# Moving the tail of each partition's last wq row onto three DMA engines, with one x_q load and separate score rows per batch

## The chip, the cores and the metric

One core of a Trainium2 chip runs the kernel. The metric is the device time of one execution in microseconds (us). Within a set both kernels ran on the same chip; in the third set 11 of the 12 runs of the kernel before are those of the second set. A span is shorter than the metric by some 1.8 us, because it counts from the first to the last instruction of the program.

In the views, PE is the matmul engine (PEld its weight loads), DVE and ACT are the vector and scalar engines, POOL is a fourth engine, and SP (SyncE) issues the large loads; a name with q behind it (SPq, ACTq) is an engine's instruction queue, and L93 is line 93 of the kernel. Apart from these there are sixteen DMA engines, here called engine 0 to 15 (the traces do not number them), which move the data. Of their queues, q1 carries the weights and caches, q10 the small x loads and the output, and q8 and q14 carry instructions.

## The reference, cut to what matters

One decode step for four sequences: layer norm, q projection, sliding-window attention over 2048 cached positions, output projection, then a gated MLP.

```python
def reference(A_x, A_k_cache, A_v_cache, A_wq, A_wo, B_x, B_w1, B_w3, B_w2):
    # B=4, D=1024, Hq=32, Hkv=4, Dh=128, W=2048, F=3584, all bf16
    xn = layernorm(A_x)
    q = xn @ A_wq                                  # wq: 1024 x 4096, 8.4 MB
    k, v = A_k_cache[:, :, -W:], A_v_cache[:, :, -W:]   # 8.4 MB each
    p = softmax(q . k * Dh ** -0.5)                # each batch has its own scores
    h = A_x + (p . v) @ A_wo                       # wo: 8.4 MB
    hn = layernorm(h)
    return h + (silu(hn @ B_w1) * (hn @ B_w3)) @ B_w2   # 7.3 MB each
```

The weights and caches are 55.6 MB, each byte is used once, and all of it must come through the DMA queue.

## The kernel before

All large loads are issued by SyncE into one SBUF ring, in the order of a plan. Partition p of the wq tile holds rows 8p to 8p+7 of wq, one after another, so the "last wq row" of a partition is row 8p+7.

```python
    def load_rows(at, src, n, r0, m):
        t = ring[:, at : at + m * n]
        nc.sync.dma_start(out=t, in_=src[:, r0 * n : (r0 + m) * n])
        return [t[:, k * n : (k + 1) * n] for k in range(m)]
    plan = [
        ("wq", load_rows, (0, wq_v, N_Q, 0, 4)),
        ("wq", load_rows, (32 * KIB, wq_v, N_Q, 4, 4)),
        ("k", load_kv, (64 * KIB, A_k_cache, 0)),
        ...
    ]
    ...
    for j in range(JG):                       # x_q: the residual, in four DMAs
        nc.scalar.dma_start(
            out=x_q[QD * j : QD * (j + 1) : RS, :], in_=x_flat[:, j * CG : (j + 1) * CG])
    ...
    for kc in range(KC):                      # q projection, KC = 8
        wq_t = loaded["wq"][kc]
        for hf in range(CQ // 512):
            for g in range(JG):               # four column groups of the array
                c0 = g * CQ + hf * 512
                nc.tensor.matmul(q_ps[QD * g : QD * g + B, hf * 512 : (hf + 1) * 512],
                    lhsT=xnT[:, kc, :], rhs=wq_t[:, c0 : c0 + 512],
                    start=(kc == 0), stop=(kc == KC - 1))
        if kc == RQ - 1:
            load_next()
    ...
            nc.tensor.matmul(                 # scores
                scores_ps[QD * g : QD * (g + 1), n * 512 : (n + 1) * 512],
                lhsT=qz[:, b, g * QD : (g + 1) * QD], rhs=kT_v[:, g, :, :],
                start=(b == 0), stop=(b == B - 1))
```

## Time and profile before

| | before |
|---|---|
| time, median of the 6 runs beside the changed kernel | 138.34 us (138.11 to 138.45) |
| span of the profiled run | 136.34 us |
| q1 packets' share of 16 engines' span | 95.3% |
| landing of the last w2 load | 132.97 us |
| landings of that load, engine by engine | eight at 131.12 to 131.62, eight at 132.35 to 132.97 us |

The prediction below shows the lines on the bound. (In its line of DMA digits each digit is the busy share of the sixteen engines in one fortieth of the span, in tenths.) Two more views matter. The first is a part of the list of DMA issues (target and source, issuing engine, count, KB each, us to landing where known), the second the waits of SyncE's own queue (who waited for what: us in total, times, longest).

```profile
ring<-in_A_wq_dram SPq DMA_DIRECT2D x2, 4096.0 KB, 16.8
...
x_q<-in_A_x_dram ACTq DMA_DIRECT2D x4, 2.0 KB
```

```profile
SPq L101 <- DMA ring<-in_A_wq_dram: 16.2, 2, 9.9
```

Line 101 issues the K and V loads. It waits for wq although K has nothing to do with wq. In the trace's instruction records each DMA posts its completion to one of eight semaphores, in turn, and a DMA whose semaphore is still in use must wait until the earlier DMA has landed. The third K load got the semaphore of the first wq load and was issued at 13.02 us, when that landed. It cost nothing, for the second wq load and two K loads were queued by then.

### The profile page before, as it was taken

How to read it: one execution, taken by the hardware profiler on the slowest of the kernel's cores; microseconds unless marked ns; L12 is line 12 of the kernel's file. 1: busy time of each engine (PE TensorE's matmuls, PEld its weight loads, DVE VectorE, ACT ScalarE, POOL GpSimd, SP SyncE). 2: the span in 40 equal slices, each digit the busy share in tenths (PEclk: the TensorE clock that was granted, in tenths of full speed). 3: DMA queues.
4: the chain of work that ended last, by engine and by line, in shares of the span. 5: the costliest groups of instructions: out<-in, count | busy, mean ns of one | idle time of the engine just before them, and what ended most of it. 6: DMA issues, size and time to landing. Idle time of an engine off the chain costs nothing.

```text
span 136.3 us, 2302 instructions
## 1 busy us (share of the span) xinstructions
PE 67.9 (50%) x1035; PEld 42.9 (31%) x1035; DVE 42.6 (31%) x73; ACT 31.0 (23%) x36; POOL 1.7 (1%) x8
## 2 busy tenths in 40 slices
PE   0101803698989889105259538830096440900960
PEld 0100201274656565001149427610043210300840
DVE  6440000244444444609940030160000695070000
ACT  0400000155555646092944000000003300000001
POOL 5000000000000000000000000000000000000000
PEclk9999999999999999965555865897557777555577
DMA  5999899999999999997988989989799999989960
GB/s 156 462 462 443 385 413 418 423 447 423 428 437 409 437 437 423 435 582 341 538 385 365 524 365 442 459 353 522 328 412 463 434 437 447 429 388 409 426 261 5
DMA packets 2662, 55.75 MB, mean 409 GB/s; under 512 B 312, under 2 KB 344, under 8 KB 604
## 3 DMA queue, kind: packets, MB, share of 16 engines
q1 hardware_dynamic: 2592, 55.58, 95.3%
q8 instruction: 8, 0.13, 0.3%
q10 hardware_dynamic: 60, 0.02, 0.1%
q14 instruction: 2, 0.02, 0.0%
HBM read 55.59 MB, written 0.01 MB: 408 GB/s over the span
## 4 chain that ended last, share of the span: by engine, by line
DMA 58%; PE 21%; ACT 13%; DVE 5%; issue 1%; SPq 0%; ACTq 0%
DMA ring<-in_B_w_dram 42%; DMA ring<-in_A_wq_dram 16%; PE kt_ps L263 9%; ACT kT L269 6%; PE scores_ps L248 5%; ACT z L304 3%; PE q_ps L215 2%; PE g_ps L403 2%; DVE rmax L280 2%; ACT Pm L285 2%; PE OT_ps L326 2%; DVE pT L294 1%; DVE z L300 1%; ACT L285 1%; DVE q_sb L225 1%
## 5 line engine op out<-in xcount | busy, mean ns | idle before, releaser
L269 ACT COPY kT<-kt_ps 128x1024 bf16<-128x1024 bf16 x16 | 15.8, 1014 | 12.0 <-PE kt_ps L263 12.0
L263 PE MATMUL kt_ps<-ident,ring 128*128 128x128 bf16 x256 | 16.4, 219 | 0.0
L263 PEld LDWEIGHTS <-ring 128*128 128x128 bf16 x256 | 14.3, 98 | 5.0 <-issue 4.9
L267 DVE COPY kT<-kt_ps 128x1024 bf16<-128x1024 bf16 x16 | 11.1, 691 | 15.2 <-PE kt_ps L263 15.2
L215 PE MATMUL q_ps<-ring,xnT 128*4 128x512 bf16 x64 | 6.7, 596 | 12.0 <-DMA ring<-in_A_wq_dram 12.0
L403 PEld LDWEIGHTS <-hnT 128*32 128x32 bf16 x128 | 5.3, 137 | 23.1 <-issue 20.5
L248 PE MATMUL scores_ps<-kT,qz 128*32 128x512 bf16 x64 | 9.9, 609 | 3.1 <-ACT kT L269 3.1
L326 PE MATMUL OT_ps<-z,ring 128*128 128x32 bf16 x256 | 7.4, 185 | 6.7 <-ACT z L304 5.0
L403 PE MATMUL u_ps<-ring,hnT 128*32 128x448 bf16 x64 | 6.3, 572 | 8.3 <-DMA ring<-in_B_w_dram 8.3
L403 PE MATMUL g_ps<-ring,hnT 128*32 128x448 bf16 x64 | 5.4, 525 | 9.0 <-DMA ring<-in_B_w_dram 9.0
L433 PE MATMUL y_ps<-ring,hgT 128*32 128x256 bf16 x112 | 5.7, 370 | 8.4 <-DMA ring<-in_B_w_dram 8.3
L326 PEld LDWEIGHTS <-ring 128*128 128x128 bf16 x256 | 7.3, 103 | 7.4 <-issue 7.4
L433 PEld LDWEIGHTS <-hgT 128*32 128x32 bf16 x112 | 4.4, 129 | 10.3 <-issue 6.1
L215 PEld LDWEIGHTS <-xnT 128*4 128x4 bf16 x64 | 2.1, 116 | 16.2 <-issue 15.9
L353 PE MATMUL y_ps<-ring,o 128*32 128x256 bf16 x128 | 5.8, 365 | 2.0 <-DMA ring<-in_A_wo_dram 2.0
L443 ACT CAST res<-y_ps 128x256 bf16<-128x256 f32 x1 | 0.4, 372 | 26.5 <-PE y_ps L433 26.5
L304 ACT ACTIVATE z<-pt_ps,mask 128x512 bf16<-128x512 f32 x8 | 5.3, 687 | 3.5 <-DVE z L300 3.5
L225 DVE TENSOR_SCALAR q_sb<-q_ps 128x512 bf16<-128x512 f32 x1 | 0.7, 690 | 17.2 <-PE q_ps L215 17.2
L353 PEld LDWEIGHTS <-o 128*32 128x32 bf16 x128 | 4.8, 130 | 3.8 <-issue 3.1
L300 DVE TENSOR_SCALAR z<-pt_ps,mask 128x512 bf16<-128x512 f32 x8 | 5.5, 740 | 1.2 <-ACT z L304 0.8
L296 PE MATMUL pt_ps<-pT,perm 128*128 128x512 bf16 x4 | 2.4, 607 | 6.8 <-DVE pT L294 6.8
L417 DVE RECIPROCAL eg<-eg 128x896 f32<-128x896 f32 x1 | 5.8, 5753 | 0.0
(73 smaller groups left out, 40.5 us busy)
## 6 DMA issues: line engine op xcount, KB each, us to landing
ring<-in_A_wq_dram SPq DMA_DIRECT2D x2, 4096.0 KB, 16.8
ring<-in_A_k_cache_dram SPq DMA_DIRECT2D x4, 2048.0 KB, 25.5
ring<-in_A_v_cache_dram SPq DMA_DIRECT2D x4, 2048.0 KB, 40.2
ring<-in_B_w_dram SPq DMA_DIRECT2D x1, 7168.0 KB
ring<-in_B_w_dram SPq DMA_DIRECT2D x2, 3584.0 KB, 28.6
ring<-in_B_w_dram SPq DMA_DIRECT2D x1, 4352.0 KB
ring<-in_B_w_dram SPq DMA_DIRECT2D x1, 1792.0 KB
ring<-in_B_w_dram SPq DMA_DIRECT2D x1, 768.0 KB
```

Of the source, the lines that this page charges most:

```text
L215: nc.tensor.matmul(q_ps[QD * g : QD * g + B, hf * 512 : (hf + 1) * 512], lhsT=xnT[:, kc, :], rhs=wq_t[:, c0 : c0 + 512], start=(kc == 0), ...
L248: nc.tensor.matmul(scores_ps[QD * g : QD * (g + 1), n * 512 : (n + 1) * 512], lhsT=qz[:, b, g * QD : (g + 1) * QD], rhs=kT_v[:, g, :, :], ...
L263: nc.tensor.transpose(out=kt_ps[:, jj, :], in_=k_v[:, n * NJ + t * TB + jj, :], identity=ident[:])
L267: nc.vector.tensor_copy(out=kT[:, t * TB : (t + 1) * TB, :], in_=kt_ps[:])
L269: nc.scalar.copy(out=kT[:, t * TB : (t + 1) * TB, :], in_=kt_ps[:])
L300: nc.vector.tensor_scalar(out=z[:, :, g, :], in0=pt_ps[:], scalar1=mask[:, g : g + 1], scalar2=None, op0=ALU.mult)
L304: nc.scalar.mul(out=z[:, :, g, :], in_=pt_ps[:], mul=mask[:, g : g + 1])
L326: nc.tensor.matmul(OT_ps[:, b, :], lhsT=loaded["v"][b][:, j, :], rhs=PTz[j // NJ][:, (j % NJ) * B + b, :, :], start=(j == 0), stop=(j == J ...
L353: nc.tensor.matmul(y_ps[QD * j : QD * (j + 1), :], lhsT=o4[:, i, :, :].rearrange("p b s -> p (b s)"), rhs=loaded["wo"][i][:, j * CG : (j + ...
L403: nc.tensor.matmul(out_ps[QD * j : QD * (j + 1), hf, :HF], lhsT=hnT[:, k, :], rhs=loaded[kind][k][:, c0 : c0 + HF], start=(k == 0), stop=( ...
L417: nc.vector.reciprocal(out=eg[:], in_=eg[:])
L433: nc.tensor.matmul(y2_ps[QD * j : QD * (j + 1), :], lhsT=hgT[:, i, :], rhs=loaded["w2"][i][:, j * CG : (j + 1) * CG], start=False, stop=(i ...
```

## The change

The intent: the completion of a load needs all sixteen DMA engines, and some have spare time at the end. So 768 B are cut from each partition's last wq row, on all engines alike, and the cut pieces (128 of them) are gathered by three DMAs whose shape confines them to engines 0 to 2. The q projection adds the gathered pieces by eleven small matmuls, which use the matching rows of xn. The x_q load becomes one DMA in place of four. The score matmul takes its weights from a window that is shifted by 8 columns per batch, so that each batch has rows of its own. (Before, the four batches were summed in the same rows; the comparison with the reference accepted both kernels.)

```diff
+    CE = 384
+    SETS = [(0, 3, 5), (60, 3, 5), (120, 2, 1)]
+    def load_side(r0, ne, ns):
+        t = ktpool.tile([P, JG * QD * 16], BF16, tag="kT")
+        rows = A_wq[r0 * KC : (r0 + ne * 4 * ns) * KC, N_Q - CE : N_Q]
+        rows = rows.rearrange("(t i k) n -> k i t n", i=ne, k=KC)[KC - 1]
+        nc.sync.dma_start(out=t[: ne * 4, : ns * CE], in_=rows)
+        return [t[: ne * 4, k * CE : (k + 1) * CE] for k in range(ns)]
+    def load_tail(at, src, n, r0, m):
+        t = ring[:, at : at + m * n]
+        nc.sync.dma_start(out=t[:, : m * n - CE], in_=src[:, r0 * n : (r0 + m) * n - CE])
...
-        ("wq", load_rows, (32 * KIB, wq_v, N_Q, 4, 4)),
+        ("side", load_side, SETS[0]),
+        ("side", load_side, SETS[1]),
+        ("side", load_side, SETS[2]),
+        ("wq", load_tail, (32 * KIB, wq_v, N_Q, 4, 4)),
...
-    for j in range(JG):
-        nc.scalar.dma_start(
-            out=x_q[QD * j : QD * (j + 1) : RS, :], in_=x_flat[:, j * CG : (j + 1) * CG]
-        )
+    nc.scalar.dma_start(out=x_q[0:P:RS, :], in_=x_flat.rearrange("b (j c) -> j b c", j=JG))
...
+    (eleven slices of xn are gathered by 3 DVE copies, transposed on PE, copied to xsT)
...
+                n = min(512, N_Q - CE - c0) if kc == KC - 1 else 512
...
         if kc == RQ - 1:
             load_next()
+            for k, np_ in enumerate(sl):
+                nc.tensor.matmul(
+                    q_ps[QD * (JG - 1) : QD * (JG - 1) + B, CQ - CE : CQ],
+                    lhsT=xsT[:np_, k, :], rhs=loaded["side"][k], start=False, stop=False)
...
-                lhsT=qz[:, b, g * QD : (g + 1) * QD],
+                lhsT=qz_v[:, z0 : z0 + QD],
```

(The line in brackets stands for the part that prepares xsT.)

## The prediction

> **What bounds the kernel now.** I read the page's head, its DMA digits and queues first, then the chain of waits, the groups, the timeline of the last stretch and the SyncE queue's own waits. The page says that DMA is busy nearly everywhere and moves 55.75 MB at 409 GB/s over the whole span:
>
> ```profile
> DMA  5999899999999999997988989989799999989960
> DMA packets 2662, 55.75 MB, mean 409 GB/s; under 512 B 312, under 2 KB 344, under 8 KB 604
> q1 hardware_dynamic: 2592, 55.58, 95.3%
> q8 instruction: 8, 0.13, 0.3%
> q10 hardware_dynamic: 60, 0.02, 0.1%
> q14 instruction: 2, 0.02, 0.0%
> ```
>
> Queue q1 carries all weights and caches: 18 DMAs of 128 rows plus one completion packet on each of 16 engines give 18 x 144 = 2592 packets. It alone fills 95.3% of the engines' span. The chain names 58% DMA, but it follows the compute in the middle; it begins and ends on DMA:
>
> ```profile
> 1.16 21.35 DMA ring<-in_A_wq_dram
> ...
> 101.59 31.37 DMA ring<-in_B_w_dram
> ...
> 133.01 0.32 PE y_ps L433 x4
> ...
> 133.35 0.37 ACT res L443
> ```
>
> Behind the last landing stand only four matmuls, one copy and the 8 KB output, so the end is the landing at 132.97 us plus about 3.4 us. In the middle, PE arrives before its data and not after it:
>
> ```profile
> PE q_ps L215 <- DMA ring<-in_A_wq_dram: 12.0, 2, 6.1
> PE g_ps L403 <- DMA ring<-in_B_w_dram: 9.0, 1, 9.0
> PE y_ps L433 <- DMA ring<-in_B_w_dram: 8.3, 3, 7.1
> PE y_ps L353 <- DMA ring<-in_A_wo_dram: 2.0, 1, 2.0
> ```
>
> And each large load is issued before the queue runs dry: the timeline has the first w1 load issued at 73.22 us, while wo, the load ahead of it, lands at 82.1 us. So the queue has 8.9 us of spare time there, and wo, issued at 39.74, still more.
>
> The deciding detail is in the trace's packet records (start, duration, size, queue; no engine number). A packet starts within some 10 ns of the end of the one before it, so they link into sixteen gap-free sequences of the same 144 q1 data packets each. Every sequence is busy from about 2 us to its end, and the ends fall into two groups: eight at 130.78 to 131.32 us and eight at 132.05 to 132.67 us. The late eight are exactly those into which an instruction packet fell before the end: seven q8 packets of 16 KB (starting at 31.2, 42.1, 52.5, 75.4, 82.2, 88.5, 106.5 us; 0.88 to 0.96 us each) and one q14 packet at 57.9 us. Each costs its engine some 1.3 us for good. The eighth q8 packet starts at 131.11 us, on an engine already done. A load has landed only when its slowest engine has, so **the latest instruction-hit engine sets the time**, and eight others idle for the last 1.3 us.
>
> **What the Trainium skill says.** "DMA: Bandwidth & Descriptors", section "Why a DMA increments its semaphore by 16 and not by 1": a DMA is split over the largest k up to 16 that divides the slowest dims of both sides, on this issue path over the lowest-numbered k engines. The trace fits: q10 has x_sb (4 data and 4 completion packets), four x_q loads (4 and 4 each) and the output (16 and 4), 8 + 32 + 20 = 60, so four-row copies run on four engines. The change's side loads have outer sizes 3 against 12, 3 against 12, and 2 against 8: engines 0 to 2, 0 to 2 and 0 to 1. Same page, "Queues, rings and completion order": an engine alternates between queues packet by packet, and completion is counted over all engines; in the trace the 512 B x_q packets start 2.45 us apart (6.04, 8.49, 10.94), always after large packets end. Same page, "Rules for kernel authors": a DMA with a small outermost size is confined to that many engines. Here that is the intent.
>
> **The change part by part.**
>
> *Bytes taken off all engines.* The second wq load shrinks by 384 x 2 = 768 B on each of 128 partitions, 8 of them per engine: 6144 B. A 32 KB packet takes 1.21 us (27.1 B per ns), so each engine ends 6144 / 27.1 = 0.227 us sooner. The packet count per engine stays 8.
>
> *Bytes put on engines 0 to 2.* The same 128 pieces come back as 60 + 60 + 8 packets of 768 B: 20 + 20 + 4 = 44 on engines 0 and 1, 40 on engine 2. For a packet this small I take the line through two sizes of this trace: successive 2048 B packets start 80 ns apart, 32,768 B ones 1211 ns, so 4.6 ns + 0.0368 ns per byte, 32.9 ns for 768 B (512 B packets took 27 ns, which agrees roughly). 44 x 32.9 = 1.45 us, with three completions of about 15 ns 1.49 us; less 0.227, **engines 0 and 1 end 1.27 us later**; engine 2, 40 x 32.9 = 1.32, plus 0.03, less 0.227: 1.12 us later. That is nearly the 1.3 us for which an engine without an instruction packet idles. So the author has filled three of the idle tails.
>
> *The end.* Engines 3 to 15: latest 132.67 - 0.23 = 132.44 us. Engines 0 to 2, if unhit: 130.78 to 131.32 plus 1.12 to 1.27, so 131.9 to 132.6 us. The sequences that carry the x_q packets, and so belong to engines 0 to 3, can be followed with some ambiguity where packets tie: three seem unhit (ends near 131.01, 131.08, 131.32), one hit. I choose to believe that engine 3 is the hit one, since the change stops at 2. Then the last data end at 132.44 to 132.59 instead of 132.67: **0.08 to 0.23 us gained, 0.15 as the middle.**
>
> *Earlier landings.* The second wq load waits for engines 0 to 2: they were somewhere in 21.98 to 22.51, and become about 23.2 to 23.7 us. The q matmuls and the whole attention start about 1.1 us later, as does the first K landing (27.4). Attention's slack against wo is 2.0 us (the wait above), so some 0.9 us is left. The w1 issue moves from 73.2 to 74.3 with 8.9 us of slack. Nothing at the end moves.
>
> *Added compute.* DVE gets three small strided copies and two out of PSUM, by the 0.17 us of the similar 128x32 copy about 0.9 us; PE eleven transposes (eight take 0.66 us, so 0.9 us). Both lie between 7.3 us and the wq landing at 13.0, where they idle. Eleven side matmuls of 384 columns share one column group: four 512-column ones side by side take 3.58 / 8 = 0.45 us, so each needs 0.34 us and all 3.7 us, from 16.6 to 20.3 us; wq1 comes after that.
>
> *x_q in one DMA.* Three issues of 0.58 us leave ACT's queue, and its table load, now at 3.94 us, starts earlier; xnT is ready at 7.2 us for data that come at 13.0. Worth nothing. With three DMAs more on SyncE the number of DMAs in this phase is the same, so the completion semaphores go round as before: SyncE holds K and V back until earlier loads have landed, but a full queue stands ahead.
>
> *Score rows.* Another 32-column slice of qz per batch: the same 64 matmuls (609 ns) and weight loads. It changes what the rows contain, not the time.
>
> **The rivals.** (1) *An instruction packet on engine 0, 1 or 2.* The mapping of sequences to engine numbers is inferred. If a hit engine is among them, it ends at 132.67 + 1.2 = 133.9 and the kernel takes about 139.6 us. The added 44 PE instructions also move the eighth q8 packet forward: it came after 2022 of 2078 instructions, and 44 earlier is near the end of the 68-matmul group (126.30 to 130.12 us), say 129.9. There its engine still has about 1 us of data; it becomes a ninth late engine, near 132.2, harmless unless it is one of 0 to 2. (2) *Small packets cost more than the line says.* At twice 33 ns the three engines end 1.45 us later still, near 134, for 139.7 us. The 27 ns of the 512 B packets speaks against it. (3) *Moved bytes hidden anyway*: if the late engines vary from run to run, the relief is just 0 to 0.2 us, 138.4 us. (4) *PE becomes the bound* through the attention start 1.1 us later: against it stand 2.0 us of slack; if the delay were 3 us, wo's matmuls would slip by 1 us, still ahead of w1 by 8 us.
>
> **Range and chances.** Sum: 138.38 - 0.15 = 138.23, raised slightly for the one-sided risks: **138.25 us**. Below, no more than 0.23 us can be gained by the relief, and runs scatter by 0.1: low 137.95. Above, rivals 1 and 2 with about one chance in five together reach 139.6; high 139.3. A 2% limit is 2.8 us: faster 0.01, same 0.97, slower 0.02.
>
> **What would show it.** q1 should have 2592 + 128 + 8 = 2728 packets and q10 60 - 12 = 48. The wq1 landing should move later by about 1 us, the PE wait for wo shrink from 2.0 to about 1, and the last landing stay within 0.25 us of 132.97. The sixteen sequences should show three with 768 B packets 33 ns apart, ending with the late ones, so that fewer engines idle at the end. A last landing at 134, with a side engine alone at the end, would prove rival 1 or 2; a DMA gap in mid-kernel or a longer wo wait would prove the slack wrong.

## The result, and the profile after

Measured: **137.95 us** (137.82 to 138.07, 6 runs) against 138.34 us, ratio 0.9975 with a 95% interval of 0.9962 to 0.9988. A ratio here is the mean time of one kernel's runs over that of the other's in the same rounds, so it is not quite the ratio of the medians. In microseconds the ratio is a gain of 0.35, interval 0.17 to 0.53. That is "same" at the 2% limit, and lies at the lower edge of the predicted range.

The page's head of the changed kernel: DMA digits, packets and queues.

```profile
DMA  5999999999999999999989999999899999999970
DMA packets 2786, 55.75 MB, mean 409 GB/s; under 512 B 308, under 2 KB 468, under 8 KB 728
...
q1 hardware_dynamic: 2728, 55.58, 95.5%
q8 instruction: 8, 0.13, 0.3%
q10 hardware_dynamic: 48, 0.02, 0.1%
q14 instruction: 2, 0.02, 0.0%
```

The packet counts are as forecast, 2728 and 48, with the same bytes and the same mean rate. The chain that ended last (start, us, what):

```profile
3.70 19.98 DMA ring<-in_A_wq_dram
...
74.82 24.12 DMA ring<-in_B_w_dram
...
101.52 31.28 DMA ring<-in_B_w_dram
...
132.84 0.32 PE y_ps L481 x4
...
133.18 0.37 ACT res L491
```

The wq transfer now lands at 23.68 us instead of 22.51, and the last w2 load at 132.80 instead of 132.97. What follows the last landing is unchanged. The waits of the changed kernel:

```profile
PE q_ps L255 <- DMA ring<-in_A_wq_dram: 10.5, 2, 6.8
PE g_ps L451 <- DMA ring<-in_B_w_dram: 9.5, 1, 9.5
...
PE y_ps L481 <- DMA ring<-in_B_w_dram: 8.4, 3, 7.1
...
PE y_ps L401 <- DMA ring<-in_A_wo_dram: 1.3, 1, 1.3
```

PE still waits for the data of every weight matrix; its wait for wo shrank from 2.0 to 1.3 us. The added work in the timeline (start, us, engine, line, operation):

```profile
5.06 0.50 DVE L202 COPY xs<-xn 4x60 bf16<-4x60 bf16 x3
...
5.66 0.42 PE L207 MATMUL ts_ps<-ident,xs 4*12 4x4 bf16 x11
...
16.36 3.68 PE L265 MATMUL q_ps<-t,xsT 12*4 12x384 bf16 x11
```

All of it is over by 20.04 us, before the second wq load lands.

The clearest picture is in the trace's semaphore records, which hold the landing of each engine's share of a load (us, sorted; they carry no engine number):

```
second wq load, before: 16 engines 21.98 to 22.51
second wq load, after:  13 engines 21.79 to 22.28     23.41 23.55 23.68
last w2 load,   before:  8 engines 131.12 to 131.62    8 engines 132.35 to 132.97
last w2 load,   after:   4 engines 130.89 to 131.38   12 engines 132.15 to 132.80
```

Thirteen engines moved forward by some 0.2 us and three back by more than 1 us. At the end, four engines of the early group have joined the late one. By their number they are the three side engines (those that carry the side loads) and the engine with the eighth instruction packet, which now starts at 130.08 us instead of 131.11; experiment 1 checks this in a second trace. The last of all is 0.17 us earlier.

### The profile page after: what moved, and what is told of

The parts are those of the page before. It is cut to its first block, busy times and chain, and to the rows that moved or that the text cites. A ratio compares the mean times of both kernels' runs of the same rounds, so it can differ in the third digit from the quotient of the medians.

```text
span 136.2 us, 2356 instructions
## 1 busy us (share of the span) xinstructions
PE 71.4 (52%) x1057; PEld 44.1 (32%) x1057; DVE 43.2 (32%) x78; ACT 31.0 (23%) x36; POOL 1.7 (1%) x8
## 3 DMA queue, kind: packets, MB, share of 16 engines
q1 hardware_dynamic: 2728, 55.58, 95.5%
## 4 chain that ended last, share of the span: by engine, by line
DMA 55%; PE 21%; ACT 13%; DVE 5%; SPq 2%; issue 1%; ACTq 0%
DMA ring<-in_B_w_dram 41%; DMA ring<-in_A_wq_dram 15%; PE kt_ps L311 9%; ACT kT L317 6%; PE scores_ps L296 5%; ACT z L352 3%; PE q_ps L255 3%; PE g_ps L451 2%; SPq L119 2%; DVE rmax L328 2%; ACT Pm L333 2%; PE OT_ps L374 2%; DVE pT L342 1%; DVE z L348 1%; ACT L333 1%
## 5 line engine op out<-in xcount | busy, mean ns | idle before, releaser
L451 PEld LDWEIGHTS <-hnT 128*32 128x32 bf16 x128 | 5.2, 134 | 23.7 <-issue 21.0
L255 PE MATMUL q_ps<-ring,xnT 128*4 128x512 bf16 x64 | 7.2, 621 | 10.5 <-DMA ring<-in_A_wq_dram 10.5
L274 ACT ACTIVATE q_sb<-q_ps 128x512 bf16<-128x512 f32 x1 | 0.6, 597 | 23.8 <-DVE q_sb L273 23.8
```

Of the source, the lines that this page charges most:

```text
L255: nc.tensor.matmul(q_ps[QD * g : QD * g + B, hf * 512 : hf * 512 + n], lhsT=xnT[:, kc, :], rhs=wq_t[:, c0 : c0 + n], start=(kc == 0), stop ...
L451: nc.tensor.matmul(out_ps[QD * j : QD * (j + 1), hf, :HF], lhsT=hnT[:, k, :], rhs=loaded[kind][k][:, c0 : c0 + HF], start=(k == 0), stop=( ...
```

## The experiments

Twelve runs were made (two of them of the changed kernel itself), in three sets with 5 rounds each. Beside them the kernel before took 138.17 us (median of 9 runs, first set), 138.26 (11 runs, second set) and 138.22 (12 runs, third set).

Theory A: the gain is the relief of the engines that end last, and the bytes moved fit into time in which engines 0 to 2 idled at the end. Rivals: B, something else in the change brings the gain or part of it; C, it is scatter; others are named where they are tested.

### 1. The changed kernel again: r1_after and r12_after

No edit. (The diffs of the other experiments are against the changed kernel, and abridged.)

> The changed kernel itself, again, for a narrower interval. Theory A (thirteen engines are relieved by 0.23 us, and engines 0 to 2 fill their idle tail with 1.27 us): 0.1 to 0.25 us under the kernel before. Rival B (something beyond the relief also helps, as the first measurement of 0.35 us may say): 0.3 us or more. Rival C (the gain was scatter between runs): no difference.

> The changed kernel a third time, beside the three above on the same chip. 0.2 to 0.35 us under the kernel before, by the two measurements so far.

Measured: 138.03 us, ratio 0.9985 (0.9972 to 0.9999), and 138.01 us, ratio 0.9985 (0.9970 to 1.0001). With the first measurement the gains are 0.35, 0.21 and 0.21 us. The last landings of the three traces are 132.80, 132.77 and 132.86, that is 0.17, 0.20 and 0.11 us ahead of the single trace of before. Scatter (C) is unlikely, with three results on the same side, though the last interval just touches 1. Theory A's 0.15 us lies inside the second and third intervals and just under the first, whose lower end is 0.17.

The packet records of r12_after settle which engines are late. They link into sixteen sequences, as in the prediction, with every packet placed and the sizes in the order of the loads. Three sequences hold the 768 B packets (44, 44 and 40). None of these has an instruction packet before its end, and their last data end at 132.30, 132.34 and 132.44 us. The eight with an early instruction packet end at 131.78 to 132.37 us, the other five at 130.54 to 130.93. (One of the five lands late all the same: the eighth instruction packet, at 130.86 us, holds up its completion.) So in this trace a side engine is the last of all, by 0.07 us: with 384 columns the spare time of the side engines is used up.

### 2. Without the side loads: r2_no_side

```diff
-        ("side", load_side, SETS[0]),
-        ("side", load_side, SETS[1]),
-        ("side", load_side, SETS[2]),
-        ("wq", load_tail, (32 * KIB, wq_v, N_Q, 4, 4)),
+        ("wq", load_rows, (32 * KIB, wq_v, N_Q, 4, 4)),
...
-            for k, np_ in enumerate(sl):        # the side matmuls; xs and xsT go too
-                nc.tensor.matmul(q_ps[QD * (JG - 1) : QD * (JG - 1) + B, CQ - CE : CQ], ...)
```

> Of the change only the single x_q DMA and the score rows are kept; wq is loaded whole and no side loads exist. Theory A: equal to the kernel before within 0.1 us, and the last data packets end in two groups 1.3 us apart as before. Rival B (the x_q DMA or the score rows carry part of the gain): 0.1 to 0.3 us faster than before.

Measured: 138.37 us, ratio 1.0011 (0.9999 to 1.0024); the last load lands in two groups of eight again, 131.22 to 131.72 and 132.55 to 133.04 us. The gain is gone, so the other parts do not carry it. The clock's excess of 0.15 us is more than expected, and the trace places it after the kernel's work: the time from the landing of the output to the end of the span is 1.03 us, against 0.84 us before and in the changed kernel. The instruction records show why. At the end SyncE waits for the completion semaphores one after another, in the order of their numbers. In the kernel before and in the changed one the output has the last number (110), so one wait follows its landing; here the output has number 107, so four waits stand after its landing, and each further one takes some 0.06 us. The number depends on how many DMAs were issued before. (The last instruction packet, on q14, is not the cause: in this run it starts at 137.2 us, after the span has ended.) This close must be taken off before runs with different numbers of DMAs are compared by the clock: without it r2 is level with the kernel before.

### 3. Side loads alone: r3_side_only

```diff
-    nc.scalar.dma_start(out=x_q[0:P:RS, :], in_=x_flat.rearrange("b (j c) -> j b c", j=JG))
+    for j in range(JG):
+        nc.scalar.dma_start(
+            out=x_q[QD * j : QD * (j + 1) : RS, :], in_=x_flat[:, j * CG : (j + 1) * CG]
+        )
...
-                lhsT=qz_v[:, z0 : z0 + QD],
+                lhsT=qz[:, b, g * QD : (g + 1) * QD],
```

> Of the change only the side loads with their matmuls are kept; x_q comes in four DMAs and the score rows are as before. Theory A: the same gain as the changed kernel within 0.1 us. Rival B: less than the changed kernel by what the single x_q DMA and the rows bring.

Measured: **140.95 us**, ratio 1.0206 (1.0188 to 1.0223): 2.8 us slower than before. Both theories missed this. SyncE's waits and the stretch from 10 to 14 us (busy time of PE, PEld, DVE, ACT, POOL with counts, granted clock, DMA share, GB/s) of this kernel:

```profile
SPq L125 <- DMA ring<-in_A_wq_dram: 9.5, 1, 9.5
```

```profile
10.00:14.00 4.00, 0.90 (x12) 0.33 (x15) 0.00 (x0) 0.00 (x0) 0.00 (x0) 1.00 0.41 164
```

and the same stretch of the changed kernel:

```profile
10.00:14.00 4.00, 1.15 (x12) 0.38 (x15) 0.00 (x0) 0.00 (x0) 0.00 (x0) 1.00 0.99 420
```

Line 125 is the second wq load. It waited 9.5 us for the first one to land and was issued at 13.08 us. The records show why: x_sb, the first wq load, four x_q loads and two side loads had taken all eight completion semaphores, the third side load reused that of x_sb, and the second wq load that of the first. So thirteen engines had nothing to do from about 12 us, when the first load's packets ended (11.93 to 12.58 us), until the second's began (14.05 to 14.77 us). Summed over the packets from 12 to 20 us, an engine idled 1.65 us on average; and the first packets after the gap took 1.30 to 1.94 us instead of 1.19, so that the eight packets of this load cost each engine another 0.6 us. Together they are some 2.2 of the 2.8 us; like r2 the kernel also closes late, 1.07 us after the output's landing instead of 0.84, because five waits follow it. So the single x_q DMA is not tidying: it frees the three semaphores that the side loads need.

### 4. The side loads kept, no relief: r4_no_relief

```diff
-        nc.sync.dma_start(out=t[:, : m * n - CE], in_=src[:, r0 * n : (r0 + m) * n - CE])
+        nc.sync.dma_start(out=t, in_=src[:, r0 * n : (r0 + m) * n])
```

> The side loads stay, but the second wq load brings the last rows whole again, so nothing is taken off any engine (the same columns arrive twice, and the result is right). Theory A: engines 0 to 2 end at 131.0 to 131.3 plus 1.5 us, 132.5 to 132.8, the other late ones at 132.67 as before: the time equals the kernel before, at most 0.15 us above. Rival B (adding load to engines 0 to 2, or the later start of attention, itself helps): the gain stays. Rival D (the added load is not hidden): 1 us or more slower.

Measured: 138.25 us, ratio 1.0002 (0.9990 to 1.0015). Against r1_after of the same set, 138.03 us, the missing relief costs 0.22 us by the medians, which is 6144 B at 27.1 B per ns (0.227 us); the intervals are some 0.2 us to either side, so that it fits so closely is chance. The last load lands at 133.14 us, and twelve engines are late, as in the changed kernel, but 0.3 us later (four land at 131.18 to 131.56 us, twelve at 132.47 to 133.14). The relief makes the gain; the side loads by themselves make none, and cost 0.03 us by the ratio, at most 0.2 us by its interval.

### 5. Other sizes: r5_ce192 and r6_ce512

```diff
-    CE = 384
+    CE = 192     # r5
+    CE = 512     # r6, with SETS = [(0, 3, 4), (48, 3, 4), (96, 3, 2), (120, 2, 1)]; empty matmul skipped
```

> Half the columns (192 instead of 384): every engine is relieved by 384 x 8 / 27.1 = 0.113 us, engines 0 and 1 get 44 packets of 384 B, 44 x 18.7 ns = 0.82 us. Theory A: the last data of the late engines end 0.11 us before those of the kernel before, engines 0 to 2 stay some 0.6 us ahead of them, the time is about 0.1 us under the kernel before, half the gain of 384 columns. Rival B (the gain does not come from the bytes): the same gain as with 384.

> 512 columns in four side DMAs (a third more): relief 0.30 us, engines 0 and 1 get 44 x 42.3 ns = 1.86 us, net 1.56 us later. Theory A: they now end last, at about 132.6 to 132.9 us, with the others at 132.37; the time goes back to the kernel before, 0.1 us above or below it: the minimum lies near 384. Rival B (more relief is simply better): 0.3 us under the kernel before. One more DMA goes round among the completion semaphores, and if it makes a wq or K load wait for the first wq load, the time rises by 0.5 to 3 us with a gap in DMA near 13 us.

Measured: 138.01 us, ratio 0.9990 (0.9974 to 1.0007) for 192 columns, and 138.36 us, ratio 1.0013 (0.9995 to 1.0030) for 512. The intervals are too wide to tell 192 from 384, but the last landings are in the predicted order: 132.97 without, 132.87 with 192, 132.77 to 132.86 with 384, and 133.10 with 512. In the last case the sorted landings show who is last:

```
r6_ce512, last w2 load: 130.99 131.02 131.14 131.24 | 132.07 132.40 132.46 132.57 132.59 132.59 132.61 132.62 132.64 | 132.90 132.91 133.10
```

Three engines stand alone at the end, and the other late ones have moved from 132.97 to 132.64, about the forecast relief of 0.30 us. (By the clock, 0.11 us of this run's time is the close: it ends 0.94 us after the output's landing.) The three are most likely the side engines: their number fits, and the second wq load of this run, too, ends with three landings apart from the others (23.80 to 23.99 us, the rest by 22.13). More relief is not simply better: past some size the side engines become the bound.

### 6. The same pieces on other engines: r7_side16 and r8_side8

```diff
-        nc.sync.dma_start(out=t[: ne * 4, : ns * CE], in_=rows)
+        nc.sync.dma_start(out=t[:, :CE], in_=wq_v[:, KC * N_Q - CE :])   # r7: 128 rows, one matmul
...
-    SETS = [(0, 3, 5), (60, 3, 5), (120, 2, 1)]
+    SETS = [(0, 8, 4)]                                                  # r8: one DMA, 8 engines
```

> The same 384 columns come as a separate DMA of 128 rows of 768 B, so over all sixteen engines, with one side matmul. Theory A: every engine carries as much as before (eight small packets and one completion more, about 0.06 us), so the two groups of ends 1.3 us apart are back and the time equals the kernel before, 0 to 0.1 us above it. Rival B (splitting the tail off helps in itself, for instance by an earlier start of something): the gain of the changed kernel stays.

> The same pieces in one DMA over engines 0 to 7, 16 packets each: 16 x 32.9 = 0.53 us less 0.23, so 0.30 us more on each of the eight. Theory A: some of engines 3 to 7 are hit by instruction packets, and the latest of them ends at 132.67 + 0.30 = 132.97; the time is 0.2 to 0.35 us above the kernel before and 0.5 above the changed one. Rival B (it does not matter which engines carry the pieces): the gain of the changed kernel stays.

Measured: 138.52 us, ratio 1.0021 (1.0006 to 1.0036), and 138.56 us, ratio 1.0023 (1.0009 to 1.0037). By the clock neither has a gain. But part of this is the close of the program: the span ends 1.19 and 1.20 us after the output's landing instead of 0.84. Three waits stand after the landing in place of one, as in r6, and a closing instruction of ScalarE comes late, which adds some 0.23 us, for a reason that was not found. Taken off, the two are 0.04 to 0.09 us under the kernel before, with intervals of about 0.2 us to either side, so the clock alone doesn't decide. The last landings are 132.92 us in r7, in two groups of eight again (131.26 to 131.69 and 132.30 to 132.92), and 132.98 us in r8; before it was 132.97, in the changed kernel 132.77 to 132.86. So in single traces the end of the data is where it was before, and splitting the tail off brings at most a small part of the gain by itself; that the pieces must go to engines with spare time is what both traces point to. The sum for r8 does not hold at the end of the data: 133.27 us was expected (132.97 as the end of the packets; a landing is recorded 0.3 us later). So r8's time was right for a wrong reason; what its traces support is that its data end 0.12 to 0.21 us after the changed kernel's, not 0.5.

### 7. What cost r3 its time: r9_xq_late and r10_wq_first

```diff
     xn = act.tile([B, D], BF16)                 # r9, beside the edit of r3:
     nc.vector.tensor_scalar(out=xn[:], ...)
+    for j in range(JG):                         # moved to here, after the layer norm
+        nc.scalar.dma_start(out=x_q[QD * j : QD * (j + 1) : RS, :], ...)
...
+        ("wq", load_tail, (32 * KIB, wq_v, N_Q, 4, 4)),     # r10, beside the edit of r3
         ("side", load_side, SETS[0]),
         ("side", load_side, SETS[1]),
         ("side", load_side, SETS[2]),
-        ("wq", load_tail, (32 * KIB, wq_v, N_Q, 4, 4)),
...
-        if kc == RQ - 1:
-            load_next()
+        if kc == RQ - 1:
+            load_next()
+        if kc == KC - 2:
             for k, np_ in enumerate(sl):
```

> As r3_side_only (side loads, x_q in four DMAs, old score rows), which lost 2.8 us, but the four x_q DMAs are issued after the first layer norm instead of at the start. Theory A (r3 lost because the x_q and side DMAs used up the free completion semaphores, so that the second wq load waited until 13.06 us for the first to land, and the engines ran dry): the second wq load is issued by 5 us, the GB/s digits show no dip near 12 us, and the time is that of the changed kernel, 138.0 within 0.2 us. Rival E (four x_q DMAs beside the side loads cost engines 0 to 3 the 2.8 us by their packets): still 2 us or more above.

> As r3_side_only, but the second wq load is issued ahead of the side loads, and the side matmuls stand before the last wq row's. One of the later DMAs still waits for the first wq load, but with the second wq load queued. Theory A: no dip in DMA near 12 us. The side pieces land about 24 us, the q vector is ready some 3 us later than in the changed kernel and attention with it; since all loads are issued ahead of need, this costs nothing at the end or at most 0.3 us: 138.0 to 138.4. Rival F (the later attention is what cost r3 its time): 2 us or more above the kernel before.

r9 failed as an experiment: the x_q loads depend on nothing in the layer norm, the scheduler put them back to the start, and on every engine the instructions of r9 are those of r3 in the same order; only line numbers differ. It measured 140.87 us, ratio 1.0193 (1.0174 to 1.0211), which repeats r3.

r10 measured 140.02 us, ratio 1.0134 (1.0112 to 1.0156), with runs from 138.62 to 140.21. Its stretch from 10 to 14 us:

```profile
10.00:14.00 4.00, 1.08 (x12) 0.38 (x15) 0.00 (x0) 0.00 (x0) 0.00 (x0) 1.00 0.90 388
```

The gap of r3 is gone, with the same DMAs: from 12 to 20 us the packets leave no idle time, and the first engine ends wo at 79.62 us, as in the changed kernel (79.66) and not as in r3 (82.43). So up to there four x_q loads beside the side loads cost nothing (rival E falls), and what hurt r3 is which load had to wait. But r10 is slow for another reason, which neither theory held for so large. The chain:

```profile
22.22 2.73 PE q_ps L258 x24
24.95 3.60 PE q_ps L269 x11
...
79.04 20.36 DMA ring<-in_B_w_dram
```

The eleven side matmuls now stand in the path of q, attention is over later, and the first w1 load is issued at 79.04 us instead of 74.82. In this trace the engines end wo from 79.62 us on, and the earliest w1 packet starts at 80.00: an engine idles 0.13 us on average between 78 and 84 us, and its first w1 packets take 0.31 us longer in the mean. These are 0.44 us of the 1.0 us by which the profiled run, 139.22 us, is slower than the kernel before; the close is 0.24 us more (1.08 us), and the rest was not found. The other runs were up to 1 us slower still; I take it that the gap is wider in them, but no trace shows that. So part of rival F is right: a later attention costs nothing only while the w1 load is issued about 1 us before the engines run dry.

### 8. The old score rows: r11_old_rows

```diff
-                lhsT=qz_v[:, z0 : z0 + QD],
+                lhsT=qz[:, b, g * QD : (g + 1) * QD],
```

> The changed kernel with the score rows of before. Theory A: equal to the changed kernel within 0.1 us. Rival G (the rows carry part of the gain, or cost 0.2 us): 0.2 us or more beside it.

Measured: 138.01 us, ratio 0.9983 (0.9968 to 0.9998), the same median as the changed kernel beside it. The rows cost and bring nothing.

No version beats the changed kernel clearly; r5 is level with it.

## Why the prediction was right or wrong

The time, 137.95 us against a forecast of 138.25 and a range of 137.95 to 139.3, was right, at the very edge of the range. That it came so near to falling out was most likely scatter: the same kernel took 138.03 and 138.01 us later.

**The bound and the two groups of ends** were right. r2 and r7 bring back the two groups of eight, and r6 shows a third group of three. That the instruction packets make the late group is read from traces (in that of before each of the eight late sequences has one and no early sequence has one before its end; in r12_after each of the late ones that is no side engine has one); no run took them away. The 8 KB packet cost less than the 1.3 us of the others: its engine ends at 132.04 us, some 0.5 us before the seven with 16 KB. The pages behind this: the Trainium skill, "Runtime: NRT & Kernel Launch", section "Instruction fetch mechanics", says that instructions come in 16 KiB blocks of 256 and that crossing a block is mostly hidden. The trace agrees with the blocks (eight q8 packets of 16,384 B); for the DMA engine that carries one, it is not hidden.

**The relief** of 0.227 us was right: r4 against r1 shows 0.22 us by the clock, and its last landing is 0.28 to 0.37 us after those of the changed kernel's three traces.

**The cost of the small packets** was right to the nanosecond: 768 B packets start 33 ns apart in the trace, 32.9 was worked out. The Trainium skill, "DMA: Bandwidth & Descriptors", section "Why small descriptors are slow (HBM only)", gives a fixed overhead of about 3 cycles per packet, which is 3.5 ns at the 850 MHz that the same page gives for the fabric (an estimate from that page). The line through two sizes of this trace had 4.6 ns. The measured 33 ns fit the line; with 3.5 ns the same slope gives 31.8 ns.

**The later landing of wq** was forecast as 23.2 to 23.7 us and is 23.68; the issue of w1 as 74.3 and is 74.82; the eighth instruction packet as 129.9 and is 130.08; PE's wait for wo as about 1 and is 1.3 us.

**The size of the gain.** The step was "0.08 to 0.23 us gained, 0.15 as the middle". The last landings in three traces say 0.11 to 0.20 us. The clock says 0.35, 0.21 and 0.21 us. They agree within the intervals, except that the first interval begins at 0.17. Whether there is another 0.1 us beyond the relief stays open; neither the rows (r11) nor the single x_q load with the rows (r2) bring it. It is below what these rounds resolve.

**Which engine was hit** was a choice, "I choose to believe that engine 3 is the hit one". It came out right, and this was luck as far as the prediction goes. In r12_after no side engine has an early instruction packet; had one carried such a packet, the last landing would be near 134 us, and in no trace of the changed kernel is it above 132.86. Rivals 1, 2 and 4 of the prediction did not come to pass.

**Wrong or undervalued.** Two steps were off, though neither mattered for the number. First, "Worth nothing" for x_q in one DMA: by itself it is, but r3 shows that the side loads without it lose 2.8 us. The prediction saw that the number of DMAs stays the same, and did not ask what would happen if it did not. Second, "the queue has 8.9 us of spare time" ahead of w1: it was counted to the landing of wo, 82.1 us. The engines begin to run dry earlier, at 79.86 us in the trace of before, and a load needs about 1 us from its issue to its first packet (0.96 us for w1 in r10, 0.97 us for the second wq load in r3). The slack was 79.86 - 1.0 - 73.22 = 5.6 us, not 8.9. The changed kernel used 1.6 of it; r10 used all.

## What to carry to other kernels

When a kernel is bound by DMA throughout, look at the landings of the last load engine by engine: the slowest engine is the bound, and what can be gained is the mean idle time at the end, here 0.9 us of 138 (132.97 less the mean of the sixteen landings, 132.08), of which the confined side loads won 0.11 to 0.20 by the landings and 0.21 to 0.35 by the clock. Count completion semaphores when adding DMAs near the start: one more can make a large load wait for another to land, which cost some ten times what the balance brought (2.8 us in r3). Measure the slack of an issue to the moment the first engine runs dry, less the time from issue to first packet, not to the landing of the load ahead.

## What the Trainium skill lacked or had wrong

- "Runtime: NRT & Kernel Launch", "Instruction fetch mechanics", calls the block crossing mostly hidden. For the instruction stream that may be so; in this kernel, bound by DMA, each block holds up the DMA engine that carries it: 16 KB packets of 0.88 to 0.96 us, and the mean landing of the eight hit engines (seven with 16 KB, one with 8 KB) is 132.76 us against 131.40 us for the others, 1.36 us later.
- "DMA: Bandwidth & Descriptors", "Rules for kernel authors", advises a shape that uses all 16 engines and says that transfers under 64 KB pay mostly overhead. Here 45 KB loads confined to three engines, behind a running queue, cost 33 ns per 768 B packet (23 B per ns against 27 for large ones) and, with as many bytes taken off all engines, the kernel became faster by 0.2 to 0.35 us; with the pieces spread over all 16 engines (r7) the last load landed at 132.92 us, against 132.97 before.
- No page that I read gives the cost of restarting drained engines: in r3 the first 32,000 B packets after a gap took 1.30 to 1.94 us instead of 1.19.
- No page that I read tells that the close of a program depends on which completion semaphore the output has: SyncE waits for them in the order of their numbers, and each wait after the output's takes some 0.06 us. From the output's landing to the end of the span: 0.84 us with one wait (before, changed kernel), 0.94 with three (r6), 1.03 with four (r2), 1.07 with five (r3). In r7 and r8, with three, it is 1.19 and 1.20, of which some 0.23 us is a late closing instruction of ScalarE, with no cause found.
